# Two packed attentions and a squared-ReLU MLP on one core: the written-out order of all engines replaced from layer 1's first product on

## The chip, the core and the metric

The kernel runs on one core of one Trainium2 chip. Its engines are TensorE (PE; its weight loads, PEld, overlap its matmuls), VectorE (DVE), ScalarE (ACT), GpSimd (POOL), SyncE (SP), and 16 DMA engines that serve queues fed by POOL, SP and ACT. Each engine works through its own list of instructions in the order in which they were written, and waits where an instruction needs a result of another engine. The metric is device microseconds of one execution; a time is the median of several.

## What is computed

Eight batches and eight heads, 576 positions, head dimension 64, 32 packed rows. Two attentions stand behind each other, then a two-layer MLP over all 4608 tokens (512 to 2048 to 512).

```python
def sm_attn(qq, kk, vv):
    s = scale * np.matmul(qq, kk.transpose(0, 1, 3, 2))
    s = s - np.max(s, axis=-1, keepdims=True)
    a = np.exp(s)
    a = a / (np.sum(a, axis=-1, keepdims=True) + 1e-09)
    return np.matmul(a, vv)
p_packed = sm_attn(p, k, v)
out = sm_attn(q, p_packed, p_packed)
...
h = x @ w_in
r = np.maximum(h, 0.0)
g = r * r
return (g @ w_out).astype(np.float32)
```

The kernel does not form the second attention's output. It multiplies the packed values with w_in first (`wp`), and layer 1 is then `wp` times the second softmax.

## The kernel before

All work is cut into words, and the string `ORDER` (line 50) lists all 1451 of them. `run` (L768) takes word after word, and `step` (L738) hands each to a method that issues its instructions. Every engine's sequence is thus the sequence of its words in `ORDER`; between engines only data dependences, buffers and the waits that follow from them order the work. A letter behind a colon chooses the engine: v for VectorE, a for ScalarE, p for GpSimd; without one it is VectorE.

The words that matter here, with b the batch, qd one of two groups of four heads, hf one of two parts of the 576 positions:

- `Lk`, `Lv`, `Lq` (`LA`, `LB` for parts of q), `Wi`, `Wo`, `Pr`: loads, issued on POOL's DMA queue. `Wo0` to `Wo3` are the quarters of w_out (L261).
- `kT`, `qT` (`qA`, `qB`): transposes on DVE. `s1`: first scores on PE (L375). `m1`: their maximum on DVE (L401). `x1`: exponential on ACT (L413). `eT`, `eo`: transpose on PE and its copy. `pv`, `pp`, `bd`, `bs`, `pt`, `po`: packed values and their layouts.
- `s2` (`zA`, `zB`): second scores. `t2`, `m2`, `sb`, `x2`, `su`, `a2`, `aT`: the second softmax, ending in `a2T`. Batches 0 and 1 do it in two cuts (tA, mA and so on).
- `w0`, `w1` (`wa`, `wb`), b, qd: packed values times a part of w_in on PE (L574). `W0`, `W1`, `Wa`, `Wb`: the copy out of PSUM (L419 on ACT, L421 on DVE). `w1` and `W1` give the columns that fb 4 to 7 and 12 to 15 need.
- `h`b.hf.fb: one 128-row block of layer 1, two matmuls (L590). `r`b.hf.fb: its relu out of PSUM (L595 on ACT, L597 on DVE). `q`b.hf.fp: the square of two such blocks into `gT` (L633 on ACT, L635 on DVE or POOL).
- `o`tt.j: two of the 16 matmuls of output tile tt (128 tokens, L648). `c`tt: the copy to `o_sb`. `d`tt: its store, issued on SP (L679).
- `Z`: filler matmuls on PE ahead of layer 1.

PSUM has eight banks. `psa` holds two tiles of two banks for scores, transposes and `wp`; the pools `x` and `y` have two banks each. An `h` of batches 1 to 7 takes a `y` bank; in batch 0 blocks of even fb take `x`, odd ones `y`. Output tiles take `x`, tiles 0 and 1 `y`. A product may start when the relu or copy of an earlier holder of its bank is done. SBUF pools are as short: six `r` tiles, five `o_sb`, three k tiles, two of most softmax tiles.

The matmuls differ in the tile of the array that they use: 128x128 for `h`, `o`, `eT` and `pt`; 32x32 for scores; 64x32 for `w`; 96x32 or 128x32 for `pv`.

Of the kernel before, what the change touches and what calls it, by code (L numbers as in the profile page):

```python
# [65 lines left out]
h1.0.3 c3:a o4.0 r1.0.3:v r1.0.4:a o5.0 kT20 q1.0.1:a h1.0.7 d3 h1.0.5 uB10 o5.1 r1.0.5:a o4.1 r1.0.7:v q1.0.2:a aB10
h1.0.10 h1.0.8 q1.0.3:v r1.0.10:a o4.2 kT21 Lq2 h1.0.9 r1.0.8:a o5.2 r1.0.9:a h1.0.12 TB10 s12 q1.0.4:v r1.0.12:a
h1.0.14 m120 o5.3 Lv30 r1.0.14:a h1.1.1 m121 h1.1.3 r1.1.1:a o5.4 x120 r1.1.3:v h1.0.11 o4.3 r1.0.11:v x121 h1.1.7 kT31
h1.0.15 eT20 Lq3 q1.0.5:a o4.4 r1.0.15:v eT21 r1.1.7:v q1.0.7:a o5.5 rd2 eo20:v eo21:a h1.0.13 h1.1.2 r1.0.13:v o4.5
r1.1.2:v q1.0.6:a h1.1.6 pv2 r1.1.6:v h1.1.8 pp2 h1.1.0 q1.1.1:a r1.1.8:v Lk30 o5.6 qT21 q1.1.3:a o4.6 h1.1.12 r1.1.0:a  # L70
bd2 pt2 qT20 o4.7 bs2:a Lk40 h1.1.5 po2:v r1.1.12:a o5.7 q1.1.0:v c4:a h1.1.10 r1.1.5:v c5:a s22 d4 r1.1.10:v h1.1.4
o6.0 t221 r1.1.4:a h1.1.9 d5 o7.0 q1.1.2:a t220 h1.1.13 r1.1.9:a o6.1 qT30 r1.1.13:a Lq4 h1.1.11 q1.1.4:a m221 w120 w121
r1.1.11:a o6.2 m220 W121:a h1.1.14 h1.1.15 W120:v Lv31 o6.3 r1.1.14:a q1.1.6:a o7.1 o6.4 sb21:v r1.1.15:a Lv40 o7.2
q1.1.5:a kT30 o7.3 q1.1.7:a o7.4 sb20:v Lk41 x221 o6.5 qT31 o7.5 x220 o6.6 su21 o6.7 o7.6 su20 c6:a o7.7 w020 a221 c7:a
d6 w021 o8.0 W020:a a220 o8.1 d7 o8.2 aT21 W021:a o8.3 aT20 o8.4 Lq5 h2.0.1 h2.0.0 r2.0.1:v o8.5 r2.0.0:a o8.6 q2.0.0
h2.0.2 h2.0.3 r2.0.2:v o9.0 Lk50 o8.7 r2.0.3:v h2.0.5 c8:a s13 q2.0.1 r2.0.5:a h2.0.4 d8 m130 o10.0 r2.0.4:a h2.0.6 kT40
h2.0.7 r2.0.6:a o10.1 r2.0.7:a q2.0.2 h2.0.10 Lk51 x130 m131 o9.1 h2.0.8 r2.0.10:a q2.0.3 o9.2 r2.0.8:a kT41 h2.0.13
x131 eT30 h2.0.9 r2.0.13:v o10.2 eo30:a rd3 r2.0.9:v h2.1.1 eT31 q2.0.4 h2.0.14 r2.1.1:a o10.3 r2.0.14:v eo31:a h2.0.11
Lk61 o9.3 r2.0.11:v o9.4 h2.0.12 h2.1.5 q2.0.5 r2.0.12:a pv3 r2.1.5:v h2.0.15 q2.0.6 h2.1.4 pp3 r2.0.15:a o9.5 r2.1.4:v
h2.1.6 bd3 pt3 q2.0.7 h2.1.0 bs3:a o9.6 r2.1.6:v r2.1.0:v Lv41 po3:a o9.7 q2.1.2 h2.1.8 q2.1.0 c9:a h2.1.2 r2.1.8:v s23  # L80
r2.1.2:a Lv50 d9 o11.0 t230 h2.1.3 h2.1.7 t231 o10.4 r2.1.3:a w130 m230 r2.1.7:a w030 W130:a h2.1.10 q2.1.1 h2.1.9
q2.1.3 o10.5 W030:a m231 o10.6 o11.1 sb30:v r2.1.10:a o11.2 r2.1.9:a sb31:v o10.7 x230 o11.3 q2.1.4 c10:a h2.1.15 qT40
o11.4 x231 h2.1.11 su30 r2.1.15:a w031 d10 r2.1.11:a w131 W031:a h2.1.14 su31 h2.1.13 o12.0 r2.1.14:a a230 o12.1
r2.1.13:a o12.2 W131:a q2.1.5 o12.3 a231 h2.1.12 o11.5 aT30 r2.1.12:a o12.4 aT31 o12.5 q2.1.6 q2.1.7 h3.0.5 h3.0.2 qT41
r3.0.5:a o12.6 h3.0.0 r3.0.2:v Lq6 o11.6 r3.0.0:a o12.7 h3.0.1 h3.1.1 r3.0.1:v c12:a o11.7 r3.1.1:v s14 d12 c11:a q3.0.0
h3.0.4 kT50 h3.0.3 r3.0.4:a o13.0 r3.0.3:a m140 d11 h3.0.9 Lk60 o14.0 r3.0.9:a q3.0.1 h3.1.3 x140 kT51 h3.1.0 o14.1
r3.1.3:a m141 o13.1 Lk70 r3.1.0:a h3.0.8 q3.0.2 eT40 x141 h3.0.7 r3.0.8:v o13.2 eo40:v r3.0.7:a h3.0.6 q3.1.0 o14.2
q3.0.4 r3.0.6:a eT41 rd4 q3.0.3 h3.0.11 eo41:a h3.1.2 r3.0.11:v o14.3 r3.1.2:v o13.3 h3.0.12 h3.0.10 q3.1.1 pv4
r3.0.10:a r3.0.12:v o14.4 Lv51 pp4 h3.0.13 q3.0.5 h3.0.14 r3.0.13:a bd4 o13.4 r3.0.14:v bs4:a pt4 Lv60 q3.0.6 h3.0.15
h3.1.8 o13.5 po4:v r3.1.8:a o14.5 r3.0.15:v s24 q3.0.7 h3.1.11 t240 h3.1.6 r3.1.11:a o13.6 t241 r3.1.6:a o13.7 w040 qT51  # L90
c13:a w041 h3.1.4 W040:a m241 o16.0 d13 h3.1.5 m240 r3.1.4:a o16.1 r3.1.5:a o14.6 W041:a sb41:v h3.1.9 h3.1.7 q3.1.2
o14.7 r3.1.7:a sb40:v r3.1.9:a w140 w141 x241 q3.1.3 h3.1.10 c14:v o16.2 W141:a h3.1.13 q3.1.4 d14 o15.0 su41 r3.1.10:a
o16.3 x240 o15.1 r3.1.13:v W140:a h3.1.12 q3.1.5 o16.4 a241 o15.2 r3.1.12:a h3.1.14 su40 h3.1.15 o16.5 r3.1.14:a q3.1.6
o15.3 r3.1.15:a a240 o15.4 o16.6 q3.1.7 o15.5 aT40 aT41 o16.7 qT50 o15.6 c16:a h4.0.1 h4.0.4 Lq7 r4.0.1:v o15.7 d16
r4.0.4:v o17.0 c15:a h4.0.3 h4.0.2 r4.0.3:v o17.1 r4.0.2:a d15 s15 q4.0.1 h4.0.0 kT60 h4.0.9 o17.2 r4.0.0:a m151 o17.3
r4.0.9:a h4.0.6 m150 o17.4 r4.0.6:a h4.1.3 q4.0.0 x151 o17.5 kT61 o18.0 x150 o17.6 r4.1.3:v Lk71 h4.0.5 h4.0.13 rd5
r4.0.5:a o18.1 r4.0.13:v eT50 h4.0.11 eo50:v h4.0.12 eT51 q4.0.2 o17.7 r4.0.12:v r4.0.11:a o18.2 eo51:a c17:v h4.1.2
h4.0.10 q4.0.6 r4.1.2:a pv5 d17 r4.0.10:a h4.0.7 Lv61 q4.1.1 h4.0.15 r4.0.7:a o19.0 q4.0.5 r4.0.15:a pp5 o19.1 q4.0.3
o19.2 Lv71 bd5 h4.0.8 pt5 bs5:v h4.1.11 r4.0.8:a o18.3 po5:v q4.0.4 h4.1.1 s25 r4.1.11:a r4.1.1:v o18.4 qT60 h4.1.0
o18.5 t251 h4.1.6 o19.3 r4.1.0:a t250 r4.1.6:a o18.6 q4.1.0 h4.0.14 h4.1.10 m251 r4.0.14:a w050 r4.1.10:a w150 q4.0.7  # L100
W050:a h4.1.4 m250 h4.1.7 o18.7 r4.1.4:v W150:a o19.4 r4.1.7:v o19.5 q4.1.5 c18:a o19.6 q4.1.3 sb50:v o19.7 d18 h4.1.8
qT61 c19:a o20.0 x250 h4.1.5 sb51:v o21.0 d19 r4.1.5:a o20.1 r4.1.8:a su50 o21.1 x251 h4.1.12 q4.1.2 h4.1.9 r4.1.12:a
w151 a250 r4.1.9:a w051 h4.1.15 W151:a su51 o20.2 o21.2 r4.1.15:a q4.1.4 o21.3 W051:a a251 o20.3 h4.1.14 aT50 h4.1.13
aT51 s16 r4.1.14:a r4.1.13:v o20.4 kT70 h5.0.6 h5.0.8 r5.0.6:a m160 o20.5 r5.0.8:a h5.0.0 q4.1.7 o21.4 x160 m161 h5.0.4
o21.5 r5.0.0:a q4.1.6 eT60 r5.0.4:a kT71 h5.0.9 h5.0.1 x161 o20.6 r5.0.9:v o20.7 eo60:v r5.0.1:a h5.0.5 rd6 q5.0.4 c20:a
# [717 lines left out]
```

## Time and profile before

| | us |
|---|---|
| median of 3 runs | 243.22 (242.80 to 243.59) |
| the profiled execution | 243.35 |
| its span, first to last instruction | 241.5 |
| granted TensorE clock | 0.999 |

The page gives busy time by engine, then the costliest groups; the trace behind it gives every instruction's start, its idle time and what ended it. Idle time of an engine that is not the bottleneck costs nothing by itself.

### The profile page before, as it was taken

What the parts mean: (1) busy time and instruction counts of PE and PEld (TensorE: products, weight loads), DVE (VectorE), ACT (ScalarE), POOL (GpSimd) and SP (SyncE); (2) the same over time, 40 slices, a digit from 0 to 9 for tenths busy, and PEclk for the clock granted to TensorE, in tenths of its full rate; (3) what the DMA queues carried; (4) which work ended last, traced back from release to release, by engine and by line L of the source; (5) the groups of instructions that cost most, each with busy time, mean ns of one, the idle gap of its engine ahead of it and who ended that gap; (6) DMA issues with size and microseconds to landing.
All of it is one profiled execution on the core that took longest, in us unless ns stands there. A gap on an engine that the chain in (4) does not pass through costs nothing.

```text
span 241.5 us, 6098 instructions
## 1 busy us (share of the span) xinstructions
PE 235.4 (97%) x2415; PEld 125.9 (52%) x2415; DVE 203.0 (84%) x459; ACT 142.0 (59%) x308; POOL 74.8 (31%) x123
## 2 busy tenths in 40 slices
...
GB/s 103 189 199 210 202 206 206 181 209 210 194 169 212 236 103 136 51 71 209 107 86 28 206 107 66 62 34 105 37 24 76 46 46 43 43 46 43 50 61 109
DMA packets 33404, 28.51 MB, mean 118 GB/s; under 512 B 8160, under 2 KB 28384, under 8 KB 33376
## 3 DMA queue, kind: packets, MB, share of 16 engines
...
q14 instruction: 9, 0.07, 0.1%
q10 hardware_dynamic: 144, 0.07, 0.1%
...
## 4 chain that ended last, share of the span: by engine, by line
PE 91%; DMA 4%; ACT 2%; DVE 1%; SPq 0%; issue 0%; POOL 0%; POOLq 0%
PE ps_o L648 50%; PE ps_h L590 26%; PE ps_wp L574 4%; PE ps_idle L335 3%; PE ps_s L375 3%; DMA k_b<-in_k_dram 2%; PE ps_e1T L433 2%; PE ps_pv L457 1%; DMA out_dram<-o_sb 1%; ACT r L595 1%; ACT wp L419 1%; SPq L679 0%; PE ps_ppT L496 0%; ACT gT L633 0%; DVE kT L351 0%
## 5 line engine op out<-in xcount | busy, mean ns | idle before, releaser
L648 PE MATMUL ps_o<-w_out_bf,gT 128*128 128x512 bf16 (+1 forms) x576 | 147.3, 378 | 0.0
L590 PE MATMUL ps_h<-a2T,wp 128*128 128x288 bf16 (+2 forms) x512 | 89.9, 286 | 1.3 <-DVE rs L543 0.6
L595 ACT ACTIVATE r<-ps_h 128x288 bf16<-128x288 f32 (+2 forms) x159 | 61.0, 415 | 47.2 <-PE ps_h L590 42.5
L648 PEld LDWEIGHTS <-gT 128*128 128x128 bf16 x576 | 54.4, 98 | 43.1 <-issue 3.4
L590 PEld LDWEIGHTS <-wp 128*128 128x128 bf16 x512 | 47.7, 98 | 42.4 <-issue 8.0
L597 DVE TENSOR_SCALAR r<-ps_h 128x288 bf16<-128x288 f32 (+2 forms) x97 | 41.9, 447 | 11.1 <-PE ps_h L590 10.5
L635 DVE TENSOR_TENSOR gT<-r 128x576 bf16<-128x576 bf16 (+2 forms) x104 | 45.1, 446 | 2.8 <-ACT r L595 1.8
L419 ACT CAST wp<-ps_wp 128x1024 bf16<-128x1024 f32 (+1 forms) x29 | 27.7, 974 | 9.0 <-PE ps_wp L574 8.9
L419 ACT COPY o_sb<-ps_o 128x512 f32<-128x512 f32 x26 | 15.2, 589 | 12.3 <-PE ps_o L648 10.1
L268 POOL DMA_DIRECT2D k_b<-in_k_dram x28 | 15.2, 544 | 16.5 <-DVE kT L351 7.3
L268 POOL DMA_DIRECT2D q_b<-in_q_dram x16 | 11.0, 690 | 28.8 <-DVE qT L363 25.4
L313 POOL DMA_DIRECT2D v_b<-in_v_dram x12 | 9.4, 779 | 31.5 <-PE ps_pv L457 30.5
L335 PE MATMUL ps_idle<-gT 128*128 128x512 bf16 (+1 forms) x59 | 16.1, 417 | 1.2 <-DVE gT L187 1.2
L413 ACT ACTIVATE e<-ps_s,nm 128x576 bf16<-128x576 f32 x16 | 11.8, 742 | 7.5 <-DVE nm L401 7.4
L633 ACT ACTIVATE gT<-r 128x512 bf16<-128x512 bf16 (+1 forms) x21 | 14.0, 690 | 0.5 <-DVE r L597 0.3
L535 ACT ACTIVATE e<-d 128x576 f32<-128x576 f32 (+2 forms) x20 | 11.7, 599 | 4.1 <-DVE d L529 3.9
L351 DVE STREAM_TRANSPOSE kT<-k_b 128x576 uint32<-128x576 uint32 x16 | 12.3, 767 | 0.6 <-DMA k_b<-in_k_dram 0.6
L363 DVE STREAM_TRANSPOSE qT<-q_b 128x576 uint32<-128x576 uint32 (+2 forms) x20 | 12.4, 633 | 0.0
L541 DVE TENSOR_REDUCE sums<-e 128x18 f32<-128x576 f32 (+2 forms) x20 | 12.2, 608 | 0.1
L401 DVE TENSOR_REDUCE nm<-ps_s 128x1 f32<-128x576 f32 x16 | 11.5, 739 | 0.8 <-PE ps_s L375 0.7
L523 DVE TENSOR_REDUCE mx<-s 128x18 f32<-128x576 f32 (+2 forms) x20 | 11.6, 609 | 0.0
L529 DVE TENSOR_TENSOR d<-s,mx 128x576 f32<-128x576 f32 (+2 forms) x19 | 11.6, 631 | 0.0
...
## 6 DMA issues: line engine op xcount, KB each, us to landing
...
v_b<-in_v_dram POOLq DMA_DIRECT2D x12, 256.0 KB, 5.5
w_out_bf<-in_moe_w_out_dram POOLq DMA_DIRECT2D x4, 512.0 KB, 12.4
...
w_in_bf<-in_moe_w_in_dram POOLq DMA_DIRECT2D x4, 256.0 KB, 9.8
```

What stands on the lines that cost most here:

```text
L268: engine.dma_start(x[n:], s[:P - n])
L335: self.nc.tensor.matmul(ps[:, :m], lhsT=self.nought[:, :P], rhs=self.nought[:, :m], start=True, stop=True)
L351: self.nc.vector.transpose(t["kT"][:].rearrange("p s e -> p (s e)").bitcast(U32), t["k"][:].rearrange("p t d -> p (t d)").bitcast(U32))
L363: self.nc.vector.transpose(out.bitcast(U32), x.bitcast(U32))
L419: engine.copy(out, x)
L541: nc.vector.reduce_sum(out=sums[:, x], in_=t["e2"][:, x], axis=AX.X)
L590: self.nc.tensor.matmul(ps, lhsT=t["wp"][:, fb // n, fb % n * P:(fb % n + 1) * P], rhs=t["a2T"][:, s0:s1], start=(qd == 0), stop=(qd == se ...
L595: engine.activation(r, ps, ACT.Relu)
L597: engine.tensor_scalar_max(r, ps, 0.0)
L633: engine.activation(out, r, ACT.Square)
L635: engine.tensor_tensor(out=out, in0=r, in1=r, op=ALU.mult)
L648: self.nc.tensor.matmul(self.o[tt][:, e], lhsT=self.gT[:, fb, a:a + P], rhs=self.w_out_bf[:, fb, e], start=(i == 0), stop=(i == self.NFB - 1))
```

## The change

`ORDER` is replaced. The 1451 words are the same; the first 83, up to and with `h0.0.8`, stand as before. From there on the sequence of every engine is new, many words change their engine, and loads and stores change places in their queues. All squares of batches 2 to 7 were on VectorE; now half of them carry `:a`. Nothing else in the file differs.

The first lines that differ, and some further places:

```diff
-sB00:p Wa01:a TA01 Z1.1 wb01 TA00 Lv10 wb00 xB00 sB01:v h0.0.8 h0.0.9 Wb01:a Wb00:v h0.0.1 h0.0.0 xB01 uB00 r0.0.8:a
-r0.0.1:a h0.0.2 uB01 r0.0.9:a aB00:p r0.0.0:a h0.0.3 r0.0.2:v q0.0.4:a h0.0.11 Wo2 aB01:v h0.0.10 q0.0.0:a TB00 TB01
-r0.0.3:a r0.0.10:v r0.0.11:a h0.1.0 h0.1.1 q0.0.1:v q0.0.5:a h0.1.9 r0.1.0:v h0.1.8 r0.1.1:a r0.1.9:v LA1 w100 w101
-q0.1.0:v r0.1.8:a h0.1.10 W100:v W101:a h0.1.11 h0.1.3 q0.1.4:p h0.1.2 r0.1.10:a r0.1.3:v r0.1.11:a h0.0.4 kT10 r0.1.2:a
-LB1 h0.0.13 r0.0.4:a h0.0.5 q0.1.1:a h0.1.14 r0.0.13:v q0.1.5:p h0.0.14 r0.0.5:v h0.1.13 r0.1.14:a kT11 h0.0.15
-r0.0.14:a h0.0.6 q0.0.2:a h0.0.12 Wo1 r0.0.15:v s11 r0.1.13:a r0.0.12:v r0.0.6:a Wo3 h0.1.15 q0.0.7:v q0.0.6:a h0.0.7
-r0.1.15:v h0.1.4 r0.0.7:a Lv20 h0.1.6 m110 r0.1.4:a h0.1.5 r0.1.6:a h0.1.7 m111 h0.1.12 q0.0.3:a o2.0 x110 r0.1.5:v o2.1
-r0.1.12:v q0.1.7:p o0.0 x111 o3.0 r0.1.7:a eT10 q0.1.6:a o0.1 Pr q0.1.2:v eT11 q0.1.3:v eo10:a o1.0 rd1 eo11:v o3.1 pv1
...
+mA00 sA01:v xA01 sA00:v uA01 xA00 qB00 Wo0 qB01 aA01:p uA00 Z18.1 zB0 wa00 Lv11 tB00 tB01 aA00:p Wa00:a mB00 Z2.1 wa01
+mB01 sB00:p Wa01:a TA01 Z1.1 wb01 TA00 Lv10 wb00 xB00 sB01:v h0.0.8 Wb01:a h0.0.0 xB01 Wb00:v r0.0.0:a h0.0.1 uB00
+uB01 h0.0.9 h0.0.2 aB00:p r0.0.1:a h0.0.11 r0.0.2:v r0.0.8:a aB01:v r0.0.9:a TB00 h0.0.3 q0.0.0:a TB01 LA1 r0.0.11:a
+h0.0.10 w100 r0.0.10:v h0.1.8 h0.1.1 r0.0.3:a q0.0.4:a W100:v h0.1.9 h0.1.0 r0.1.8:a r0.1.1:a h0.1.10 w101 r0.1.9:v
+h0.1.3 q0.0.5:a r0.1.10:a r0.1.0:v h0.1.2 q0.1.4:p W101:a Wo2 r0.1.3:v r0.1.2:a h0.1.11 LB1 q0.1.0:v kT10 h0.0.4
+h0.0.5 Wo1 h0.0.14 r0.1.11:a r0.0.4:a q0.0.1:v r0.0.5:a h0.0.13 h0.1.14 r0.0.14:a h0.1.13 h0.0.12 r0.1.14:a r0.0.13:v
+h0.0.15 q0.0.2:a r0.0.15:a h0.0.6 kT11 r0.0.6:a q0.1.1:v s11 q0.0.7:v h0.1.15 r0.1.13:a h0.1.4 q0.1.5:p h0.1.5 m110
+r0.0.12:a o2.0 r0.1.15:a m111 x110 r0.1.5:v x111 o1.0 o2.1 h0.0.7 r0.1.4:a r0.0.7:v eT10 eT11 h0.1.7 h0.1.6 o1.1
+eo10:v rd1 eo11:a pv1 r0.1.7:v r0.1.6:a h0.1.12 pp1 o0.0 q0.1.2:v pt1 r0.1.12:a qA11 o0.1 q0.0.6:v po1:a o3.0 w011
+q0.1.7:p w111 Wo3 o2.2 bd1 q0.1.3:a W011:a o0.2 qA10 o2.3 q0.1.6:a w010 W111:v zA1 qB10 qB11 tA11 q0.0.3:a o3.1 tA10
...
+t221 o4.7 m220 Lv30 o5.7 q1.1.2:a c4:v r1.1.10:a sb20:v h1.1.12 h1.1.7 m221 w120 r1.1.12:a w121 h1.1.9 c5:a o6.0
+r1.1.7:a o7.0 sb21:v r1.1.9:a q1.1.5:v o7.1 Lk51 q1.1.3:a kT31 o6.1 o7.2 h1.1.13 h1.1.15 o7.3 x220 W120:a su20 W121:a
+o6.2 w020 r1.1.13:a q1.1.4:v w021 q1.1.6:v a220:v x221 h1.1.14 o6.3 o6.4 o7.4 o6.5 su21 r1.1.15:a W020:a a221:v
...
-o34.2 o34.3 o33.7 o34.4 c33:v o34.5 o34.6 o34.7 d33 o35.0 c34:v o35.1 o35.2 d34 o35.3 o35.4 o35.5 o35.6 o35.7 c35 d35
...
+o34.1 o33.3 r7.1.12:v o34.2 q7.1.6:a o34.3 o33.4 o34.4 o33.5 o33.6 o33.7 o34.5 o34.6 o34.7 c33:a o35.0 o35.1 o35.2
+c34:a o35.3 o35.4 o35.5 o35.6 o35.7 d33 d34 c35 d35
```

The count of words by engine, where it differs:

| words | ACT before, after | DVE before, after |
|---|---|---|
| q, batches 2 to 7 | 0, 48 | 96, 48 |
| q, batches 0 and 1 | 21, 15 | 8, 14 |
| r, batches 2 to 7 | 121, 137 | 71, 55 |
| r, batches 0 and 1 | 38, 48 | 26, 16 |
| W0, W1 | 26, 22 | 4, 8 |
| c (without c35) | 26, 28 | 9, 7 |
| eo | 7, 5 | 9, 11 |
| po | 3, 4 | 5, 4 |
| bs | 4, 2 | 2, 4 |

More of the change, by code (lines that the diff above doesn't have):

```diff
@@ L66 @@
[L66 to L105, printed above, removed]
@@ L131 @@
-o34.2 o34.3 o33.7 o34.4 c33:v o34.5 o34.6 o34.7 d33 o35.0 c34:v o35.1 o35.2 d34 o35.3 o35.4 o35.5 o35.6 o35.7 c35 d35
+pf Lk00 Lk01 Lv00 Lv01 I P0 LA0 P1 Wi00 kT00 Wi10 LB0 Z18.0 s100 Wi01 kT01 Wi11 m100 Z2.0 s101 x100 m101 Wi21 x101
+Z7.0 eT00 eo00:v Z1.0 eT01 rd0 eo01:v Wi20 Z2.0 pv0 pp0 qA01 Lk10 Z2.0 pt0 bd0 qA00 po0:a Z2.1 zA0 Lk11 tA00 tA01 mA01
+mA00 sA01:v xA01 sA00:v uA01 xA00 qB00 Wo0 qB01 aA01:p uA00 Z18.1 zB0 wa00 Lv11 tB00 tB01 aA00:p Wa00:a mB00 Z2.1 wa01
+mB01 sB00:p Wa01:a TA01 Z1.1 wb01 TA00 Lv10 wb00 xB00 sB01:v h0.0.8 Wb01:a h0.0.0 xB01 Wb00:v r0.0.0:a h0.0.1 uB00
@@ new lines @@
+o2.6 Lk20 h1.0.1 h1.0.0 Lv20 kT21 o3.3 o3.4 r1.0.0:a uB10 r1.0.1:v h1.0.3 h1.0.2 aB10:v Px o2.7 r1.0.3:a r1.0.2:a o3.5
+Pt h1.0.5 Lv21 q1.0.0:v h1.0.14 Pu q1.0.1:a xB11 r1.0.5:a o3.6 c2:a o3.7 d2 Lq2 h1.0.6 r1.0.14:v h1.0.4 Lk30 uB11 kT20
+o5.0 c3:a o4.0 r1.0.4:a r1.0.6:a h1.0.10 h1.0.11 TB10 aB11:v r1.0.10:a r1.0.11:v q1.0.2:a s12 h1.0.12 r1.0.12:v m120
+d0 h1.0.8 r1.0.8:v o4.1 m121 o5.1 o5.2 q1.0.5:a h1.0.13 h1.0.9 q1.0.3:a r1.0.9:v TB11 x120 r1.0.13:a qT21 o4.2 o4.3
+h1.1.1 h1.1.6 Lq3 x121 eT20 eT21 q1.0.4:v r1.1.1:a h1.1.0 r1.1.6:a h1.1.2 q1.0.6:v eo21:v d1 o5.3 r1.1.0:a r1.1.2:a
```

95 lines of the change are left out of this document (63 added, 32 removed).

## The prediction

> **What bounds the kernel now.** First the top of the page and the stretches of busy time (columns: stretch, its length, then busy microseconds and count for PE, PEld, DVE, ACT, POOL, then granted clock, DMA share, GB/s).
>
> ```profile
> span 241.5 us, 6098 instructions
> ...
> PE 235.4 (97%) x2415; PEld 125.9 (52%) x2415; DVE 203.0 (84%) x459; ACT 142.0 (59%) x308; POOL 74.8 (31%) x123
> ```
> ```profile
> 21.28:30.51 9.23, 7.95 (x75) 4.79 (x68) 9.07 (x22) 9.12 (x24) 6.62 (x8) 1.00 1.21 206
> 30.51:50.00 19.49, 19.49 (x253) 9.74 (x253) 16.11 (x44) 12.84 (x27) 11.99 (x20) 1.00 1.34 191
> 50.00:100.00 50.00, 50.00 (x548) 27.01 (x546) 45.93 (x96) 39.16 (x83) 26.23 (x45) 1.00 1.03 177
> ...
> 150.00:200.00 50.00, 50.00 (x547) 26.95 (x546) 45.06 (x101) 29.09 (x65) 1.38 (x2) 1.00 0.27 55
> 200.00:238.00 38.00, 38.00 (x242) 21.30 (x240) 28.03 (x62) 14.87 (x33) 0.00 (x0) 1.00 0.21 49
> ```
>
> From 30.51 us, where s11 (batch 1's first scores) starts, to 238, PE is busy every moment at full clock. A busy PE can still be a stretched one, so I next read the chain of waits for the pace of uninterrupted pieces.
>
> ```profile
> 39.87 1.40 PE ps_o L648 x6
> 43.68 5.29 PE ps_o L648 x24
> 48.96 0.44 PE ps_h L590 x4
> 88.20 0.49 PE ps_h L590 x4
> ```
>
> 24 output matmuls take 5.29, or 0.22 each, so an o word (two) costs 0.43. An h word costs 0.22 at 256 columns, 0.245 at 288, and by width 0.27 at 320. The piece of six that follows a weight product of another tile shape takes 1.40 where six cost 1.30: a change of tile shape costs 0.1. Beyond these changes nothing is lost behind 30.5. What is lost lies in the first 9 us of layer 1, shown by PE's timeline (start, length, instruction, in brackets the idle time before it):
>
> ```profile
> 21.28 1.03 PE L590 MATMUL ps_h<-a2T,wp 128*128 128x256 bf16 x8
> 22.90 1.20 PE L590 MATMUL ps_h<-a2T,wp 128*128 128x256 bf16 x8 [0.58 <-DVE rs L543]
> 24.45 1.56 PE L590 MATMUL ps_h<-a2T,wp 128*128 128x320 bf16 x8 [0.35 <-DVE a2T L563]
> ...
> 28.04 2.54 PE L590 MATMUL ps_h<-a2T,wp 128*128 128x256 bf16 x18 [0.29 <-ACT r L595]
> 30.51 0.70 PE L375 MATMUL ps_s<-kT,pT 32*32 32x192 bf16 x48
> ```
>
> Ahead of s11 stand 15 h words of 256 and 10 of 320 columns (3.3 + 2.7), w100 and w101 (0.46) and two changes of shape (0.2): 6.6 us in a stretch of 9.23. So 2.6 us is all that any order can win here, and the kernel's profiled execution (243.35, of which 241.5 is span and 1.85 lies around it; 0.13 above the median of 243.22) can hardly fall below 240.7.
>
> **The change part by part.** Both orders hold the same 1451 words, so every matmul and every transfer stays. From h0.0.8 on, three things change: each engine's sequence, the engine of some words, and the sequence of loads and stores.
>
> *Shapes.* From the product before h0.0.8 on I count 75 changes of shape in the old order and 77 in the new. The extra two come from w100 and w101 being parted, inside the stalled stretch. From s11 on both have 73. Cost on the path: 0.
>
> *Engines.* 48 squares of batches 2 to 7 go from VectorE to ScalarE, with 16 relus there; in batches 0 and 1, 10 relus go the same way and 6 squares come back; 4 wp copies, 2 e1T copies and 2 bs words go to VectorE, 2 output copies and one ppT copy to ScalarE.
>
> ```profile
> L595 ACT ACTIVATE r<-ps_h 128x288 bf16<-128x288 f32 x121 | 46.9, 414 | 45.1 <-PE ps_h L590 40.7 <-issue 1.8 <-DVE qT L363 1.5
> L635 DVE TENSOR_TENSOR gT<-r 128x576 bf16<-128x576 bf16 x96 | 41.5, 445 | 2.1 <-ACT r L595 1.2
> L597 DVE TENSOR_SCALAR r<-ps_h 128x288 bf16<-128x288 f32 x71 | 30.9, 449 | 9.9 <-PE ps_h L590 9.3
> L419 ACT CAST wp<-ps_wp 128x1024 bf16<-128x1024 f32 x26 | 26.0, 1019 | 6.5 <-PE ps_wp L574 6.5
> L419 ACT COPY o_sb<-ps_o 128x512 f32<-128x512 f32 x26 | 15.2, 589 | 12.3 <-PE ps_o L648 10.1 <-DMA out_dram<-o_sb 2.1
> L535 ACT ACTIVATE e<-d 128x576 f32<-128x576 f32 x12 | 8.3, 703 | 0.2 <-DVE d L529 0.2
> L595 ACT ACTIVATE r<-ps_h 128x320 bf16<-128x320 f32 x19 | 7.9, 443 | 0.8 <-PE ps_h L590 0.8
> L633 ACT ACTIVATE gT<-r 128x512 bf16<-128x512 bf16 x12 | 7.6, 645 | 0.5 <-DVE r L597 0.3
> L633 ACT ACTIVATE gT<-r 128x640 bf16<-128x640 bf16 x9 | 6.5, 751 | 0.0
> ```
>
> A square of 576 columns on ScalarE lies between 0.645 (512) and 0.751 (640), say 0.70, against 0.445. The 48 add 33.5 us to ScalarE and take 21.4 from VectorE; the 26 relus add 11 and take 11.7; the rest come to about minus 9 and plus 8. ScalarE goes from 142 to about 177, VectorE from 203 to about 178. Both stay below PE's 235, so the loads alone cost nothing; what counts is when a relu's turn comes.
>
> The Trainium skill speaks against this part: its page "ScalarE: Activation LUTs", section "Rules for kernel authors", puts relu and mul on VectorE, not ScalarE. The trace agrees for the square (0.70 against 0.445) and not for the relu out of PSUM (0.414 against 0.449). By the rule the new order wastes 48 x 0.255 = 12 us of engine time, and the sum would be the late-ScalarE rival's below; by the rows the waste is covered.
>
> *The start.* ScalarE sets it:
>
> ```profile
> 22.47 1.20 ACT L595 ACTIVATE r<-ps_h 128x256 bf16<-128x256 f32 x4
> 23.52 1.18 ACT L633 ACTIVATE gT<-r 128x512 bf16<-128x512 bf16 x2
> ...
> 26.64 1.01 ACT L419 CAST wp<-ps_wp 128x1024 bf16<-128x1024 f32 x1
> 26.68 1.22 DVE L421 CAST wp<-ps_wp 128x1024 bf16<-128x1024 f32 x1
> ```
>
> Relus follow each other every 0.30, squares every 0.59, so back to back each saves some 0.1 of its length. h0.0.4 needs both copies W100 and W101. In the new order ScalarE does, from 22.47: nine relus, three squares, W101, that is 9 x 0.305 + 3 x 0.59 + 1.0 = 5.5, so W101 ends at 28.0, as the old pair did at 27.9; the earlier W100 only frees h0.0.4's first matmul, about 0.2. The same nine h words as before then lead to s11. Gain: 0.2, at most 0.3 (the nine cost 2.1 from 28.0 and one change of shape). Bounds: minus 0.3 to plus 0.4, if a relu comes late.
>
> *Batch 1's first softmax.* It has less cover.
>
> ```profile
> L413 ACT ACTIVATE e<-ps_s,nm 128x576 bf16<-128x576 f32 x16 | 11.8, 742 | 7.5 <-DVE nm L401 7.4
> L401 DVE TENSOR_REDUCE nm<-ps_s 128x1 f32<-128x576 f32 x16 | 11.5, 739 | 0.8 <-PE ps_s L375 0.7
> ```
>
> From s11's end to eT11 run one maximum (0.74) and two exponentials of 0.74 with an accumulator read of about 0.2 each: 2.7 with small delays between. The old order puts 4.4 us of PE work there, the new one three h, three o, h0.0.7 and eT10: 0.8 + 1.3 + 0.2 + 0.3 = 2.6. The new wait is 0 to 0.3; I take 0.2. Behind eT11 only layer-1 and output words queue, so all of it is lost.
>
> *Bank handovers behind s11.* An h or o product must wait until a relu or copy has emptied the bank it takes. For each of the 267 handovers I set PE's words between against the work that the order lists for the emptying engine between product and release, at the row times less the overlap. Old order: 15 are short, by 1.9 us in all, one of them by over 0.4; none cost PE anything. New order: 66 short, by 18.7, and 16 by over 0.4, together 10.6. An engine may run ahead of its place in the list, so I walked the worst. h1.1.14 waits for r1.1.13, behind c5, two relus, a square, x220, W120 and W121: from w121's end 0.59 + 2 x 0.44 + 0.75 + 0.70 + 2 x 1.02 + 0.44 = 5.4, less 8 x 0.1 is 4.6; PE has three h, seven o, w020, w021 and two changes of shape between: 0.8 + 3.0 + 0.5 + 0.2 = 4.5. It fits within 0.1. Of seven places walked so, five fit and two fall short by 0.1. Lower bound: 16 x 0.03 = 0.5, or 0 if every place fits. Upper: ahead of s11 the old order has eight places short by over 0.4, together 5.5, and lost 2.6 there, about half; half of 10.6 is 5. I take 0.9, near the walked ones.
>
> *Loads.* On POOL's queue Wo2, the issue at 23.67, is moved behind LA1 and q0.1.4 (the square at 26.65). The first two rows give size and median time from issue to landing, for issues between 18 and 50 us.
>
> ```profile
> w_out_bf<-in_moe_w_out_dram POOLq DMA_DIRECT2D x4, 512.0 KB, 12.4
> ...
> q_b<-in_q_dram POOLq DMA_DIRECT2D x1, 256.0 KB, 12.3
> ```
> ```profile
> 23.67 0.80 POOL L261 DMA_DIRECT2D w_out_bf<-in_moe_w_out_dram  x1
> ...
> 26.65 1.25 POOL L635 TENSOR_TENSOR gT<-r 128x640 bf16<-128x640 bf16 x1 [1.32 <-ACT r L595]
> ```
>
> At the 206 GB/s of the first stretch 512 KB take 2.5 of these 12.4 us; some 10 are waiting behind earlier loads. Issued 4 us later (behind the square that ran until 27.9), Wo2 still joins the same line, now behind LA1's 256 KB: 1.3 later, at about 37 if it landed at 23.67 + 12.4 = 36 before; o2.2 needs it at 37.7. Cost 0; if the 12.4 count from the issue, it lands at 40.3 and costs 2.6. Later loads move too (by the list kT30 comes some 10 us earlier, and its load with it); their cover is the DMA queue, whose share falls from 1.34 to 0.27 in the stretches above. Stores change places on SP's queue (d4 comes after d14, d17 after d20); counting tiles held, at most four of five are in use when a copy needs one, so 0; without that cover a copy would wait out a store, 3.3 in the tail's row.
>
> *The tail.*
>
> ```profile
> 234.79 3.32 DMA out_dram<-o_sb
> 238.11 0.25 ACT o_sb L661
> ```
>
> The last copy waits for a store of c33. c33 now has three o words behind it ahead of o35 instead of four, and takes 0.59 for 0.69: 0 to 0.4 later against PE's end; I take 0.2.
>
> Sum: 243.35 - 0.2 + 0.2 + 0.9 + 0.2 = 244.45, so **244.4**.
>
> **The rivals.** *The order is free.* PE stays fed everywhere as it was: only the start counts, 243.2. For it: 15 short handovers that cost nothing. Against it: four times as many.
>
> *The start is won (the faster side).* If ScalarE reaches W101 a microsecond earlier, s11 comes at 29.4 and the time is 242.2, provided nothing is lost behind; it decides at s11's start. Against it: ScalarE's thirteen steps fill 22.47 to 28.0 without a hole.
>
> *ScalarE is late behind its squares.* Relus queue behind 0.70 squares and 1.02 copies, at half the listed shortfalls: 243.35 + 5 = 248.3. Against it: VectorE ran at 92% from 50 to 100 us and PE never waited; ScalarE would run at about 80%.
>
> *Wo2 lands late.* One stall of 2.6 at o2.2: 245.9, or 246.5 with half the other losses.
>
> **How the numbers follow.** Small scattered waits 0.47 (own range 243.8 to 246), free 0.28, ScalarE late 0.13, Wo2 0.07, start won 0.05. Eight in ten: 243.0 to 247.0; half of the late-ScalarE case and most of the won start are left out. About 0.3% (0.7 us) is what a measurement of this kernel can tell from no change. Faster by more: the won start, 0.05. Within: the free case and a fifth of the forecast, 0.37. Slower: 0.58.
>
> **What would show it.** s11 should start between 30.2 and 30.5, a wait of some 0.2 should stand ahead of eT11, and PE should show idle pieces of 0.1 to 0.4 between 50 and 200 us whose releasers are relus and wp or output copies. ScalarE should be busy for about 177 us and VectorE for about 178. No such pieces at all, or one long one at an output product, would make the prediction wrong; so would s11 ahead of 29.5.

## The result, and the profile after

The changed kernel takes 244.79 us (median of 5 runs, 244.53 to 245.57), the kernel before 243.22 (5 runs beside them, 242.80 to 243.59). The ratio is 1.0071, with a 95% interval of 1.0048 to 1.0093: slower by 1.2 to 2.3 us, a little under 1%, where 244.4 had been forecast. Its profiled execution took 244.79, with a span of 242.9. One execution of a later kernel (mended_start_old_rest: 246.72 us, the profiled one, at a granted clock of 0.986) ran in a slower state and is left out of the ratio given there.

The head of the page, and the stretches in the same cuts as before (stretch, length, then busy microseconds and count for PE, PEld, DVE, ACT, POOL, then granted clock, DMA share, GB/s):

```profile
PE 236.0 (97%) x2415; PEld 126.1 (52%) x2415; DVE 185.4 (76%) x398; ACT 169.3 (70%) x369; POOL 74.7 (31%) x123
```
```profile
21.28:30.51 9.23, 7.58 (x70) 4.46 (x63) 8.64 (x19) 8.81 (x23) 5.55 (x8) 1.00 1.21 206
30.51:50.00 19.49, 18.86 (x250) 9.46 (x250) 17.27 (x44) 12.84 (x27) 13.54 (x21) 1.00 1.24 178
50.00:100.00 50.00, 50.00 (x549) 27.20 (x548) 43.51 (x93) 41.53 (x92) 22.58 (x39) 1.00 0.94 161
...
150.00:200.00 50.00, 49.92 (x534) 27.22 (x533) 38.28 (x77) 37.84 (x86) 1.36 (x2) 1.00 0.21 42
```

The clock is full throughout. PE has 0.37 us less work in the first stretch and 0.63 less in the second. From 50 us on it is busy as before, with 0.08 missing between 150 and 200. So nearly all of the loss is early. PE's timeline of the changed kernel shows where:

```profile
21.41 1.03 PE L594 MATMUL ps_h<-a2T,wp 128*128 128x256 bf16 x8
...
24.86 0.41 PE L578 MATMUL ps_wp<-w_in_bf,ppT 64*32 64x512 bf16 x8 [0.42 <-DMA w_in_bf<-in_moe_w_in_dram]
...
27.01 3.12 PE L594 MATMUL ps_h<-a2T,wp 128*128 128x320 bf16 x20
31.06 0.60 PE L594 MATMUL ps_h<-a2T,wp 128*128 128x256 bf16 x4 [0.94 <-DVE r L601]
31.59 1.04 PE L379 MATMUL ps_s<-kT,pT 32*32 32x192 bf16 x48
...
164.94 0.78 PE L594 MATMUL ps_h<-a2T,wp 128*128 128x288 bf16 x4
...
195.81 0.89 PE L594 MATMUL ps_h<-a2T,wp 128*128 128x288 bf16 x4
...
238.60 1.06 PE L657 MATMUL ps_o<-w_out_bf,gT 128*128 128x128 bf16 x16
239.70 0.27 ACT L665 COPY o_sb<-ps_o 128x128 f32<-128x128 f32 x1 [2.91 <-PE ps_o L657]
```

The same place at the end of the kernel before, from its PE timeline:

```profile
236.95 1.06 PE L653 MATMUL ps_o<-w_out_bf,gT 128*128 128x128 bf16 x16
```

Between the four marks (h0.0.8, s11, the 16 last matmuls, the end of the span) the two profiled executions compare as follows:

| piece | before | after | difference |
|---|---|---|---|
| start to h0.0.8 (same words in both) | 21.28 | 21.41 | +0.13 |
| h0.0.8 to s11 | 9.23 | 10.18 | +0.95 |
| s11 to the last 16 matmuls | 206.44 | 207.01 | +0.57 |
| from there to the end (spans are given to 0.1) | 4.5 | 4.3 | -0.2 |

That is the 1.4 us between the spans. Two waits of PE stand behind the 0.95: one of 0.94 ahead of h0.0.15 (31.06), for a relu on VectorE, and one of 0.42 ahead of w100 (24.86), for the last load of w_in. Against them stand waits that the kernel before had and this one has not; those that PE's rows list between h0.0.8 and s11 come to 1.22 before (0.58, 0.35, 0.29) and 2.11 after (0.58, 0.17, 0.42, 0.94). Of the 0.57, s11 itself is 0.34: it lasts 1.04 instead of 0.70, since it starts before the transpose kT11 is done. Two small waits can be seen as rows in which four 288-column matmuls take 0.78 and 0.89 where others take 0.65; they come to 0.37, more than the 0.23 that is left, so some 0.14 was won at other places; which ones is open.

The longer wait, ahead of h0.0.15, is for r0.0.13, the relu that empties the bank it takes. The timelines of VectorE, GpSimd and ScalarE show why this relu is late:

```profile
27.97 0.74 DVE L639 TENSOR_TENSOR gT<-r 128x640 bf16<-128x640 bf16 x1
28.63 0.77 DVE L355 STREAM_TRANSPOSE kT<-k_b 128x576 uint32<-128x576 uint32 x1
29.33 1.15 DVE L639 TENSOR_TENSOR gT<-r 128x512 bf16<-128x512 bf16 x1
30.58 0.42 DVE L601 TENSOR_SCALAR r<-ps_h 128x256 bf16<-128x256 f32 x1
31.09 0.78 DVE L355 STREAM_TRANSPOSE kT<-k_b 128x576 uint32<-128x576 uint32 x1
```
```profile
27.11 1.25 POOL L639 TENSOR_TENSOR gT<-r 128x640 bf16<-128x640 bf16 x1 [2.57 <-ACT gT L637]
28.32 0.81 POOL L265 DMA_DIRECT2D w_out_bf<-in_moe_w_out_dram  x1
29.12 0.70 POOL L272 DMA_DIRECT2D q_b<-in_q_dram  x1
29.81 0.78 POOL L265 DMA_DIRECT2D w_out_bf<-in_moe_w_out_dram  x1
30.59 1.28 POOL L639 TENSOR_TENSOR gT<-r 128x640 bf16<-128x640 bf16 x1
```
```profile
28.06 2.04 ACT L599 ACTIVATE r<-ps_h 128x320 bf16<-128x320 f32 x6
```

VectorE works without a hole, but the squares q0.1.0 (27.97) and q0.0.1 (29.33) take 0.74 and 1.15, where a square of these widths takes 0.49 and 0.42 in the kernel before. What stretches them is the main question of the experiments.

### The profile page after: what moved, and what is told of

The parts are those of the page before. It is cut to its first block, busy times and chain, and to the rows that moved or that the text cites. A ratio compares the mean times of both kernels' runs of the same rounds, so it can differ in the third digit from the quotient of the medians.

```text
span 242.9 us, 6088 instructions
## 1 busy us (share of the span) xinstructions
PE 236.0 (97%) x2415; PEld 126.1 (52%) x2415; DVE 185.4 (76%) x398; ACT 169.3 (70%) x369; POOL 74.7 (31%) x123
## 4 chain that ended last, share of the span: by engine, by line
PE 86%; DMA 9%; DVE 2%; issue 1%; ACT 1%; POOL 1%; DVEq 0%; POOLq 0%
PE ps_o L652 50%; PE ps_h L594 26%; DMA w_in_bf<-in_moe_w_in_dram 5%; PE ps_wp L578 4%; DMA gT<-in_v_dram 3%; PE ps_s L379 3%; PE ps_e1T L437 2%; PE ps_pv L461 1%; DVE gT L639 1%; DVE kT L355 1%; POOL k_b L272 1%; ACT r L599 0%; PE ps_o L657 0%; PE ps_ppT L500 0%; ACT ppd L423 0%
## 5 line engine op out<-in xcount | busy, mean ns | idle before, releaser
L652 PE MATMUL ps_o<-w_out_bf,gT 128*128 128x512 bf16 (+1 forms) x576 | 143.3, 378 | 0.0
L599 ACT ACTIVATE r<-ps_h 128x288 bf16<-128x288 f32 (+2 forms) x185 | 70.5, 414 | 37.9 <-PE ps_h L594 34.9
L594 PE MATMUL ps_h<-a2T,wp 128*128 128x288 bf16 (+2 forms) x512 | 86.1, 286 | 1.9 <-DVE r L601 0.9
L652 PEld LDWEIGHTS <-gT 128*128 128x128 bf16 x576 | 55.7, 98 | 45.2 <-issue 1.1
L601 DVE TENSOR_SCALAR r<-ps_h 128x288 bf16<-128x288 f32 (+2 forms) x71 | 31.0, 446 | 22.4 <-PE ps_h L594 22.1
L637 ACT ACTIVATE gT<-r 128x576 bf16<-128x576 bf16 (+2 forms) x63 | 41.8, 681 | 2.2 <-DVE r L601 1.9
L639 DVE TENSOR_TENSOR gT<-r 128x576 bf16<-128x576 bf16 (+2 forms) x62 | 27.4, 457 | 0.8 <-ACT r L599 0.5
L423 ACT CAST wp<-ps_wp 128x1024 bf16<-128x1024 f32 (+1 forms) x25 | 23.9, 967 | 3.0 <-PE ps_wp L578 3.0
L425 DVE CAST wp<-ps_wp 128x1024 bf16<-128x1024 f32 (+1 forms) x9 | 10.4, 1157 | 2.4 <-PE ps_wp L578 2.4
L553 DVE TENSOR_TENSOR a<-e,rs 128x576 bf16<-128x576 f32 (+2 forms) x17 | 11.9, 704 | 0.2
```

Source lines behind the costliest of these rows:

```text
L423: engine.copy(out, x)
L594: self.nc.tensor.matmul(ps, lhsT=t["wp"][:, fb // n, fb % n * P:(fb % n + 1) * P], rhs=t["a2T"][:, s0:s1], start=(qd == 0), stop=(qd == se ...
L599: engine.activation(r, ps, ACT.Relu)
L601: engine.tensor_scalar_max(r, ps, 0.0)
L637: engine.activation(out, r, ACT.Square)
L639: engine.tensor_tensor(out=out, in0=r, in1=r, op=ALU.mult)
```

## The experiments

Each was timed in 5 rounds beside the kernel before (medians of 243.22 to 243.45); the ratio is to that kernel, with its 95% interval. Times within a profile are compared from h0.0.8 on, since its start differs between executions (21.1 to 22.0).

### Which half loses: the two orders joined at s11

```diff
 new_start_old_rest: the words of the changed order up to s11
+then all words that are left, in the old order
 old_start_new_rest: the words of the old order up to s11
+then all words that are left, in the changed order
```

> The changed order up to and with s11, and behind it the old order of all words that are left. Theory A (the loss is ahead of s11): s11 at 31.6 as in the changed kernel, nothing lost behind it, 243.2 + 1.1 = 244.3. Theory B (the loss is behind s11): about 243.3.

Measured: 244.52, 1.0047 (1.0033 to 1.0061).

> The old order up to and with s11, and behind it the changed order of all words that are left. Theory A (the loss is ahead of s11): s11 at 30.5; behind it 0.6 lost in small waits and 0.25 won by the tail, so 243.5. Theory B (the loss is behind s11): 244.6 or more.

Measured: 243.48, 1.0011 (1.0000 to 1.0022). By the ratios the new start costs 1.1 us (0.8 to 1.5) and the new rest 0.3 (0 to 0.5). In the second kernel s11 lies 9.23 behind h0.0.8 and lasts 0.70, as before. Theory A holds: the loss is ahead of s11 and in s11. Behind s11 the second kernel's profile loses only 0.2 up to the last 16 matmuls, not 0.6, and the tail wins 0.2 back.

### Moving the square out of the relu's way

```diff
-r0.0.4:a q0.0.1:v r0.0.5:a
+r0.0.4:a r0.0.5:a
...
-kT11 r0.0.6:a
+kT11 q0.0.1:v r0.0.6:a
```

> The changed kernel with one word moved: the square q0.0.1 stands behind kT11 on VectorE instead of ahead of r0.0.13. Theory A (the start is lost because the relu r0.0.13 stands behind that square, which took 1.15 us): h0.0.15 no longer waits 0.94 us, the first scores s11 of batch 1 start at 30.6 to 30.8 instead of 31.6, and the time falls from 244.8 to about 243.9. Theory B (the loss lies in small waits behind s11, and whatever is won ahead of s11 is given back there): s11 comes early, but the last output product starts where it did and the time stays at 244.6 to 244.9. Theory C (another step, a relu on ScalarE, was just as late): s11 stays at 31.3 or later and the time within 0.3 of 244.8.

Measured: 244.79, 1.0061 (1.0047 to 1.0074). Nothing was won. Its VectorE, ScalarE and PE timelines:

```profile
30.32 0.42 DVE L601 TENSOR_SCALAR r<-ps_h 128x256 bf16<-128x256 f32 x1 [1.25 <-ACT gT L637]
```
```profile
29.67 0.62 ACT L637 ACTIVATE gT<-r 128x512 bf16<-128x512 bf16 x1
```
```profile
30.80 0.60 PE L594 MATMUL ps_h<-a2T,wp 128*128 128x256 bf16 x4 [1.00 <-DVE r L601]
```

VectorE now stood idle for 1.25 us, until the square q0.0.2 on ScalarE had ended (29.67 + 0.62 = 30.29). r0.0.13 is the first relu of its pair and needs a new `r` tile. There are six, and counted through the order all six are held here until q0.0.1 gives one back; without it, q0.0.2 is the next to do so. So q0.0.1 is not merely ahead of the relu in a list: the relu needs its tile. Theory A named the wrong link, and C is nearest: s11 starts at 31.33.

### What stretches the square: GpSimd's load issues, or its squares

First the loads were moved out of the way.

```diff
-h0.1.2 q0.1.4:p W101:a Wo2 r0.1.3:v r0.1.2:a h0.1.11 LB1 q0.1.0:v kT10 h0.0.4 h0.0.5 Wo1
+h0.1.2 Wo2 LB1 Wo1 q0.1.4:p W101:a r0.1.3:v r0.1.2:a h0.1.11 q0.1.0:v kT10 h0.0.4 h0.0.5
...
-h0.1.4 q0.1.5:p h0.1.5
+h0.1.4 h0.1.5
...
-q0.1.7:p w111
+q0.1.7:p q0.1.5:p w111
```

> The changed kernel with GpSimd cleared from 28.4 us on: the issues of Wo2, LB1 and Wo1 stand ahead of the square q0.1.4 on GpSimd (they stood behind it), and the square q0.1.5 is moved behind q0.1.7. VectorE's list is untouched. Theory P (VectorE's square q0.0.1 took 1.15 us because GpSimd was issuing loads in that moment): it takes 0.42 again, s11 starts at about 30.9, the time is about 244.1. Theory Q (the square is stretched by something else): it takes 1.1 again, s11 stays at 31.6 and the time at 244.8. In both, q0.1.0, which ran beside the GpSimd square q0.1.4, keeps its 0.74.

Measured: 245.74, 1.0094 (1.0078 to 1.0110). VectorE and GpSimd in its profile:

```profile
27.53 2.02 DVE L639 TENSOR_TENSOR gT<-r 128x640 bf16<-128x640 bf16 x1
...
30.17 0.38 DVE L639 TENSOR_TENSOR gT<-r 128x512 bf16<-128x512 bf16 x1
```
```profile
27.15 0.76 POOL L265 DMA_DIRECT2D w_out_bf<-in_moe_w_out_dram  x1 [0.21 <-DVE r L601]
27.93 1.27 POOL L639 TENSOR_TENSOR gT<-r 128x640 bf16<-128x640 bf16 x1
```

q0.0.1 took 0.38, as P said, but q0.1.0 now took 2.02, which neither theory had. It ended at 29.55, which is 0.35 behind the end of GpSimd's square (27.93 + 1.27 = 29.20). In the changed kernel the same pair ended at 28.71 and 28.36: 0.35 again. So VectorE's square is held while GpSimd's runs and ends 0.35 behind it. And here it was held from 27.53 or soon after, while GpSimd's row still showed a load issue until 27.91. The profiled execution took 244.95, the shortest of the six; why the median lies 0.95 above the changed kernel's it does not show.

That gave theory S: GpSimd begins a square as soon as its input is there, though its rows show load issues for longer. For q0.0.1 in the changed kernel: six relus in 2.04 us follow each other every 0.32; the second, r0.1.11, is the last input of GpSimd's q0.1.5 and ends at 28.06 + 0.32 + 0.47 = 28.85. A GpSimd square takes 1.25: to 30.10. Then 0.38 for q0.0.1: 30.48, and its row ends at 29.33 + 1.15 = 30.48. One letter tests it; the loads stay.

```diff
-q0.1.5:p
+q0.1.5:v
```

> The changed kernel with one letter changed: the square q0.1.5, which stands behind s11, goes from GpSimd to VectorE. All loads keep their places. Theory S (GpSimd begins q0.1.5 as soon as the relu r0.1.11 has ended, about 28.85, behind the load issues that its rows show until 30.59, and its reads hold VectorE's square q0.0.1 up for its own length of 1.25, to 30.1): without it q0.0.1 takes 0.42 instead of 1.15, r0.0.13 runs at 29.85, the wait of 0.94 ahead of h0.0.15 falls to 0.1 or less, s11 starts at about 30.8 and the time is about 244.0. Theory P (the load issues themselves hold the square up): it still takes 1.15, s11 stays at 31.6, the time at 244.8. In both, q0.1.0 keeps its 0.74, since q0.1.4 stays on GpSimd.

Measured: 243.94, 1.0029 (1.0011 to 1.0048). VectorE, GpSimd and PE:

```profile
27.71 0.84 DVE L639 TENSOR_TENSOR gT<-r 128x640 bf16<-128x640 bf16 x1
28.48 0.77 DVE L355 STREAM_TRANSPOSE kT<-k_b 128x576 uint32<-128x576 uint32 x1
29.17 0.38 DVE L639 TENSOR_TENSOR gT<-r 128x512 bf16<-128x512 bf16 x1
29.66 0.42 DVE L601 TENSOR_SCALAR r<-ps_h 128x256 bf16<-128x256 f32 x1
```
```profile
26.96 1.25 POOL L639 TENSOR_TENSOR gT<-r 128x640 bf16<-128x640 bf16 x1 [2.19 <-DVE r L601]
...
28.97 0.70 POOL L272 DMA_DIRECT2D q_b<-in_q_dram  x1
29.66 0.78 POOL L265 DMA_DIRECT2D w_out_bf<-in_moe_w_out_dram  x1
```
```profile
30.14 0.60 PE L594 MATMUL ps_h<-a2T,wp 128*128 128x256 bf16 x4 [0.21 <-DVE r L601]
30.66 1.03 PE L379 MATMUL ps_s<-kT,pT 32*32 32x192 bf16 x48
```

Beside the same issues of LB1 and Wo1 q0.0.1 takes 0.38. The wait ahead of h0.0.15 falls from 0.94 to 0.21, and the excess over the kernel before from 1.57 to 0.51 (243.94 against 243.43). s11 lies 9.03 behind h0.0.8. Theory P falls: the issues alone do not hold the square. The cause that S names is shown: with q0.1.5 on GpSimd q0.0.1 is held, with q0.1.5 on VectorE it is not. When GpSimd's square begins is less clear than S has it (see the last section). q0.1.0 is still held by q0.1.4 (it ends at 28.55, GpSimd's at 28.21), and s11 still lasts 1.03, since kT11 still follows r0.0.13. w100 did not wait for its load in this profile, so not all of the step from 10.18 to 9.03 is the square's; the next section parts the two.

The Trainium skill has the rule: its page "SBUF — State Buffer", section "Who interferes with whom", says that a VectorE instruction with two SBUF inputs contends with a GpSimd instruction that reads SBUF, and that the second to start is blocked until the first has ended. The trace of the changed kernel agrees for q0.1.0: GpSimd's row begins first (27.11 against 27.97), and VectorE's square ends 0.35 behind its end. The 1.15 falling to 0.38 with GpSimd's square gone shows the cause for q0.0.1. By the rows alone the order of the starts does not fit in pool_quiet: there VectorE's row begins first (27.53 against 27.93), and VectorE is held all the same.

### The tile freed early

```diff
-q0.0.4:a W100:v
+q0.0.4:a q0.0.1:v W100:v
```

> The changed kernel with one word moved: the square q0.0.1 stands ahead of the copy W100 on VectorE, in a hole of 0.29 us, so that its r tile is free early and r0.0.13 has nothing but q0.1.0 and kT10 ahead of it. Theory A (r0.0.13 was late because the r tile that it takes came free only with q0.0.1): the wait of 0.94 ahead of h0.0.15 is gone, W100 is at most 0.15 later, s11 starts at 30.7 and the time falls by 0.9 to about 243.9. Theory C (a relu on ScalarE or the copy W101 would have been as late): s11 at 31.2 or later, the time at 244.5 or more.

Measured: 244.52, 1.0047 (1.0032 to 1.0062); its profiled execution took 244.09. PE, VectorE and GpSimd:

```profile
30.49 0.85 PE L379 MATMUL ps_s<-kT,pT 32*32 32x192 bf16 x48
...
34.15 0.38 PE L594 MATMUL ps_h<-a2T,wp 128*128 128x256 bf16 x2 [0.59 <-DVE r L601]
```
```profile
30.52 1.85 DVE L639 TENSOR_TENSOR gT<-r 128x640 bf16<-128x640 bf16 x2
32.29 1.41 DVE L405 TENSOR_REDUCE nm<-ps_s 128x1 f32<-128x576 f32 x2
```
```profile
30.79 1.29 POOL L639 TENSOR_TENSOR gT<-r 128x640 bf16<-128x640 bf16 x1
```

The wait ahead of h0.0.15 is gone, as A said, and s11 comes 8.83 behind h0.0.8 instead of 10.18 (w100 did not wait here either). But the next VectorE squares (q0.1.1, q0.0.7) now run into the same GpSimd square and take 1.85 for two; the maxima and r0.1.5 behind them are late, and h0.0.7 waits 0.59 (34.15). The stall was moved by 3 us and more than half of it kept, so the time is C's, though s11 was not late.

```diff
-h0.0.10 w100 r0.0.10:v h0.1.8 h0.1.1
+h0.0.10 r0.0.10:v h0.1.8 w100 h0.1.1
```

> The kernel before this one, with w100 also moved behind h0.1.8, so that PE does not reach it ahead of the load of w_in that it needs (0.42 us of waiting at 24.86 in the changed kernel). Theory A2 (that wait shifts all that follows on PE up to s11): w100's wait falls to 0.15 or less, s11 starts at about 30.4, the time is 243.5 to 243.7. Theory C2 (the wait is swallowed, since ScalarE's chain to W101 sets the start): s11 stays where the kernel before this one has it, the time within 0.15 of it.

Measured: 244.56, 1.0042 (1.0027 to 1.0057). This edit stands on top of the one before. Neither theory was tested: in the profile of square_early w100 did not wait for its load at all. That wait was 0.42, 0.37 and 0.78 in the profiles of the changed kernel, relu_ahead and new_start_old_rest, and 0 in those of pool_quiet, square5_on_vector, square_early, squares_back and all_mended: 0.2 on average. In the old order PE reaches w100 about 1.5 us later (25.93), behind the load, which landed at 24.34.

The profiles still tell what the wait costs. squares_back, the kernel of the next section, has the changed kernel's words up to s11, and its w100 did not wait:

```profile
21.99 1.03 PE L594 MATMUL ps_h<-a2T,wp 128*128 128x256 bf16 x8
...
24.95 0.41 PE L578 MATMUL ps_wp<-w_in_bf,ppT 64*32 64x512 bf16 x8
...
31.75 1.02 PE L379 MATMUL ps_s<-kT,pT 32*32 32x192 bf16 x48
```

There s11 comes 9.76 behind h0.0.8. With the wait of 0.42 it comes at 10.18, and in new_start_old_rest, where 0.78 at w100 and 0.10 ahead of it are lost, at 10.64. So in this start the wait reaches s11 in full. The 0.95 of the changed kernel's profile can now be parted: 9.03 without the held q0.0.1 and without the wait for the load (square5_on_vector), which is 0.20 below the old 9.23; 0.73 for the held square, to 9.76; 0.42 for the load, to 10.18. Moving w100 later puts s11 at 9.04 where square_early has 8.83, so it costs as much there as the wait is worth on average; that the time stayed the same fits.

### The squares that went to ScalarE

All 48 squares of batches 2 to 7 that carry `:a` were given back to VectorE, in place; the first of them:

```diff
-q2.0.1:a
+q2.0.1:v
```

> The changed kernel with the 48 squares of batches 2 to 7 that it gave to ScalarE back on VectorE, at their places in the order; the start stays as it is. Theory E (the shift of engine time is covered: VectorE goes from 185 to about 207 us busy and ScalarE from 169 to about 136, and PE does not see it): the time within 0.3 of 244.8, the small waits behind s11 (0.57 in all) stay or fall by 0.3. Theory F (in this order the relus and copies on VectorE would now queue behind squares): PE waits behind s11 grow, their releasers are relus on VectorE, and the time rises by 1 us or more.

Measured: 251.69, 1.0340 (1.0322 to 1.0359). Page and PE's waits:

```profile
PE 236.5 (95%) x2379; PEld 126.2 (50%) x2415; DVE 200.9 (80%) x446; ACT 142.7 (57%) x321; POOL 74.7 (30%) x123
```
```profile
PE ps_h L594 <- DVE r L601: 1.7, 3, 0.9
PE ps_h L594 <- ACT r L599: 1.5, 3, 0.8
```

E falls. F has the side right; but the waits listed for relus are as much on ScalarE as on VectorE, and of VectorE's 1.7 the 0.95 ahead of h0.0.15 stands ahead of s11. VectorE at 80% loses 6.9 us here, where the kernel before ran it at 84% and lost nothing. The share of busy time does not decide; the order does. In the changed order the squares on ScalarE are no burden but what makes it work.

### Towards a faster kernel

The two small waits behind s11 were covered with an output word each:

```diff
-h5.0.10 o20.6
+o20.6 h5.0.10
...
-h6.1.3 W170:v q6.0.3:a r6.1.3:a r6.0.15:a o25.7
+o25.7 h6.1.3 W170:v q6.0.3:a r6.1.3:a r6.0.15:a
```

> The old order up to s11, the changed one behind it (as in old_start_new_rest, 243.48), with o20.6 and o25.7 drawn one place forward, ahead of h5.0.10 and h6.1.3. Theory D (behind s11 these two handovers are nearly the whole loss, and a word of other work covers each): both waits are gone and the time is 243.1. Theory H (a covered handover only moves the wait to the next product): a wait of like size stands one or two words on, and the time stays at 243.5.

Measured: 243.80, 1.0026 (1.0011 to 1.0041). PE around s27 in old_start_new_rest, then in this kernel:

```profile
194.74 0.89 PE L594 MATMUL ps_h<-a2T,wp 128*128 128x288 bf16 x4
...
196.00 0.48 PE L379 MATMUL ps_s<-qT,ppd 32*32 32x288 bf16 x32
196.41 0.66 PE L594 MATMUL ps_h<-a2T,wp 128*128 128x288 bf16 x4
```
```profile
195.75 0.48 PE L379 MATMUL ps_s<-qT,ppd 32*32 32x288 bf16 x32
196.38 0.71 PE L594 MATMUL ps_h<-a2T,wp 128*128 128x288 bf16 x4
```

In both profiles the weight product w070 starts at 192.14, so the times can be compared. s27 starts 0.25 earlier, and the product behind it 0.03: the wait moved behind s27. Theory H holds.

The same two words, with the edits of square_early and square5_on_vector, in the changed order:

> The changed kernel with four words touched: q0.0.1 ahead of W100 on VectorE (as in square_early), q0.1.5 on VectorE (as in square5_on_vector), and two output words, o20.6 and o25.7, drawn one place forward, ahead of h5.0.10 and h6.1.3, the two products behind s11 that waited longest for a relu (0.13 and 0.24 us). Theory A (the losses found are separate and add up): s11 starts 8.85 us behind h0.0.8 (10.18 in the changed kernel), the wait of 0.54 ahead of h0.0.7 that square_early showed is gone, as are the two small ones, and the time is 242.9 to 243.1, which would be the first below the kernel before. Theory G (the start keeps a loss that differs between executions, because w100 now stands where the last load of w_in lands): the profiled execution looks so, but the median is 243.5 or more.

Measured: 243.96, 1.0028 (1.0009 to 1.0047). In its profile s11 lies 8.84 behind h0.0.8 and the wait ahead of h0.0.7 is gone, but the median is that of square5_on_vector. What was won ahead of s11 (0.39 against the kernel before) was lost behind it: from s11 to the last 16 matmuls it takes 207.01, 0.57 more than the kernel before, and its tail is as long as that one's. So the losses do not add up as A had it, and which words lose it is open. G's figure came true; its cause, the load, was not shown.

Last, the mended start with the old rest, joined at s11 as in the first experiment:

> The changed order up to s11 with q0.0.1 ahead of W100, and behind s11 the old order of the words that are left, with q0.1.5 on VectorE behind h0.0.7. Theory A (with the two squares out of GpSimd's way the new start is the better one): s11 starts 8.85 us behind h0.0.8, against 9.22 in the kernel before, the old rest follows without new waits (206.1 us from s11 to o35.7), and the time is 242.9 to 243.2, 0.2 to 0.4 below the kernel before. Theory J (the old rest does not fit this start, since other r tiles and banks are held when it begins): s11 is early, but 0.3 or more is lost within 10 us behind it, and the time is 243.4 or more.

Measured: 243.48 over all twelve executions, 243.36 without the one of 246.72; 1.0005 (0.9995 to 1.0016), beside 243.22 of the kernel before: the same. A's gain did not come. J's time (243.4 or more) is met or just missed; its loss behind s11 is not shown, and neither is where s11 came, since the profile is that of the one execution. No kernel tried beat the kernel before; this one and old_start_new_rest (interval from 1.0000) cannot be told from it.

## Why the prediction was right, and where it was not

The time (244.4 for 244.79) and the side were right, but not by the sum's terms. That the figure fits is luck.

| term | predicted | measured |
|---|---|---|
| start, to s11 | -0.2 (-0.3 to +0.4) | +0.95 (-0.20, held square +0.73, load of w_in +0.42), and +0.34 in s11 |
| tile shapes | 0 | 0 (nothing seen) |
| batch 1's first softmax | +0.2 | 0 |
| bank handovers behind s11 | +0.9 (0 to 5) | about +0.2 |
| loads, Wo2 | 0 | 0 (the load of w_in stands in the start) |
| tail | +0.2 | -0.2 |

*The start failed.* The step was "ScalarE sets it": I walked ScalarE's thirteen steps and took VectorE's squares at their lengths in the old trace. ScalarE was on time: W101 ended at 28.19, or 28.06 counted from the old h0.0.8, and 28.0 was forecast. Without the two things that the walk left out, s11 came at 9.03, the forecast 0.2 below the old 9.23, though a wait of 0.21 for r0.0.13 is still in that. The first thing left out is VectorE: two of its squares are held by GpSimd's squares (0.25 and 0.73 longer), and r0.0.13 could not pass them, since the r tiles were all held. The old trace has no such case: there GpSimd's squares ran, from 26.65 and 28.63 on, beside a copy, relus and transposes of VectorE, which were not stretched, and beside the last 0.11 of a square that had begun ahead of them. I asked of the moved squares only how long they take, not beside what. The second is the load of w_in: I counted the earlier w100 as a gain and did not ask whether w_in had landed by then; *Loads* looked at Wo2 alone. In the changed kernel PE reached w100 at 24.44 and the load landed at 24.82. The bound of +0.4 came from a late relu on ScalarE alone and was too narrow. The 0.34 in s11 comes from the list, not from the late relu: kT11 stands behind r0.0.13 on VectorE, and s11 lasted 1.03 in square5_on_vector too, where that relu came 1.1 earlier, counted from h0.0.8.

*The softmax* had its cover of 2.6 us exactly; no wait stands ahead of eT11.

*The handovers* were right in kind and too large. Two of the waits sought stand between 50 and 200 us, 0.13 and 0.24, both for relus; none for a copy was seen. That they move when covered shows them to be a matter of pace at those places, not of one word. The walked places, which fitted within 0.1, were a better guide than the count of shortfalls.

*The tail* had the wrong sign, from a misread row. The last copy of the kernel before was labelled as waiting for a store, but PE's last product ends at 236.95 + 1.06 = 238.01 and the copy starts at 238.09: it waited for PE. In the new kernel the label names PE. Why the end came 0.2 earlier was not tried.

*The loads of the engines* came out at 169 and 185 us for ScalarE and VectorE, not 177 and 178. I added up lengths of instructions that overlap by some 0.1 each. It mattered little: the rival "ScalarE is late behind its squares" fell, and giving the squares back costs 6.9 us. "The order is free" is nearly true behind s11 for this order and false ahead of it. Wo2 came in time: no wait of PE names w_out.

Of the signs named, s11 between 30.2 and 30.5 did not come (31.59), nor did the wait ahead of eT11; the small pieces between 50 and 200 us did. So the forecast's number rested on handovers that were worth a quarter of what I gave them, and a loss at the start that I had excluded made up for it.
